# Routed experts with a softplus-gated FFN: VectorE splits, expert 7's block order and the queue of raw weight loads

## The chip, the cores and the metric

One Trainium2 chip; the kernel runs on one of its cores. The metric is device time in microseconds (us). Engines are named as in the profile: PE (TensorE), PEld (its weight loads), DVE (VectorE), ACT (ScalarE), POOL (GpSimd), SP (SyncE).

## The reference

Three steps, the middle and the last of which matter here:

```
x = attn(r, k, v, w, a, b)                    # a recurrence over 768 steps, 32 heads of 40
x: 3072 tokens x 320
logits = x @ w_gate + log1p(exp(x @ w_noise)) * noise          # 8 experts
top2   = the two largest of each row; weights = softmax over them
out[t] = sum over its two experts e of  weight * (relu(x[t] @ w1[e]) @ w2[e])    # 320 -> 1024 -> 320
h = out @ w_in                                # 320 -> 2048, w_in and w_out are given as float64
y = (h * tanh(softplus(h))) @ w_out           # 2048 -> 320
```

## The kernel before, in words

The program has three stages: the recurrence (`Rec`, to about 535 us), the experts (`Experts`, to about 983 us) and the final FFN (`Ffn`). Nearly all matmuls are of two operands that are each split into a high and a low part: `split` (L1084) makes the high part by a rounding copy on ACT and the low part by a subtraction, on DVE or, with `pool=True`, on POOL. A product is then three matmuls, high by high, high by low and low by high.

**Blocks.** Each expert has three blocks (`NS`) of its token list: 256 rows, 256 rows and, for the third, 256 or 384 rows, chosen at run time with `tc.If(n > BIG)` on the count of the expert (L1364 to L1371, `L1364` reads the count on every engine and `L1367` branches). Block j belongs to expert j // 3. `BLOCKS` (L754) is the order: 0, 1, 3, 4, 5, ..., 22, 23 and last 2, the third block of expert 0, for which expert 0's weights are loaded and split once more as unit 8. `p` counts places in this order.

**A block** (`block`, L1213). First layer: eight times eight matmuls (L1234) into `ph` (four buffers, each for two of the eight), then hh and hl out of it by `split` with relu (L1086 on ACT, L1088 on DVE). Second layer: for each 128 rows 24 matmuls (L1253), then the copy of y (L1259 on ACT) and at the end one store of y (L1267, SP). Between these instructions the block steps through generators, whose instructions are so woven into every engine's queue: `w2` splits the second weights of this expert in the first layer of its first block; `nxt` splits the first weights of the next expert during the second layers of the first and second block; `xt` transposes and splits the x of the next block; `more` is other work, `when` says how many steps of it are taken. `more` is the route's end (`late`, `table`) for the first experts and `Decode` for the third block of experts 1 and 2 and all blocks from expert 3 on.

**x of a block.** `ahead(p)` (L1297) issues the index load for place p + 3 (SP) and the gathers for place p + 2 (POOL, L1168), into one of three buffers, `xb[j % 3]`. Third blocks and block 2 share `xb[2]`. Block 2 stands right behind block 23 in the order, so its gathers are issued at the start of block 23 (`p + 1`), and its copy `twice` (L1201, DVE) is put behind the last hl of block 23 (`fresh=False`); otherwise the copy stands behind the first hl.

**The start** (`start`, L1279). `twice(0)`, three steps of the split of expert 0's w1 (L1179 on ACT, then L1181 and L1090), then the transposes and splits of block 0's x, a step of the route's end, and the other three steps of w1. `OPT['p1']` puts the first three w1 subtractions of expert 0 on DVE and the other three on POOL; its four w2 subtractions are on POOL (`OPT.get('pw', 1)`). For experts 1 to 7 and unit 8 the subtraction of the last 64 rows of w1 (L1181, two per expert) is on POOL, the rest on DVE. The route's end (`late`, `route`) is a chain of small DVE instructions (L857 to L975) with matmuls (L966, L967) in PE's order behind the third step of block 0's second layer.

**Zero stores.** `clear` (L1157) stores zeros over the rows of `yb` of each expert's possible third group of 128 and of the overflow blocks, by SP (L1160), three or four DMAs per expert, after its second block.

**Decode** (L1400). The float64 words of w_in and w_out come as pairs of int32. 44 items of 128x256 words, four steps each: step 0 issues the load of the next item's words (L1434, SP; 52 DMAs in all, as some items have two) and three DVE instructions (L1454 to L1456), steps 1 and 2 two more each (L1458, L1459; L1461, L1462), step 3 one on DVE (L1465), the cast on ACT (L1470) and two on POOL (L1471, L1472), and for w_out two stores (L1474, L1475, SP). There are two buffers of raw words.

Of the kernel before, what the change touches and what calls it, by code (L numbers as in the profile page):

```python
# [734 lines left out]
N, DM, NE, F = 3072, 320, 8, 1024  # L735
NT = N // 128
BT = 256
NS = 3
NBS = NE * NS
BIG = NS * BT  # L740
CAP = BIG + 128
# [9 lines left out]
LW = (2, 2, 2), (2, 2, 2)  # L751
EARLY = 2 * BT

BLOCKS = [0, 1, *range(NS, NBS), 2]  # L754
AT = {j: p for p, j in enumerate(BLOCKS)}
SHUT = 2
DFF = 2048
# [335 lines left out]
class Experts:  # L1093
# [78 lines left out]
    def split_w1(self, u, to=None):  # L1172
        nc = self.nc
        a = self.ld[u][0]
        h1, l1 = self.ws[u] = to or (self.w1h(), self.w1l())
        pool = iter(OPT['p1'] if u == 0 else (u <= NE, 0, 0) * 2)
        for c in range(0, F, 512):
            f = slice(c, c + 512)
            nc.scalar.copy(out=h1[0:64, 2, f], in_=a[0:64, 2, f])  # L1179

            (nc.gpsimd if next(pool) else nc.vector).tensor_tensor(out=h1[64:128, 2, f], in0=a[0:64, 2, f], in1=h1[0:64, 2, f].bitcast(F32), op=ALU.subtract)  # L1181
            yield
            for k in range(2):
                split(nc, a[:, k, f], h1[:, k, f], l1[:, k, f], pool=next(pool))
                yield
        if u + 1 <= NE:
            self.load_w1(u + 1)

    def split_w2(self, u):

        b = self.ld.pop(u)[1]
        for m in range(0, FC, 2):
            split(self.nc, b[:, m:m + 2], self.w2h[:, m:m + 2], self.w2l[:, m:m + 2], pool=u == 0 and OPT.get('pw', 1))
            yield
        if u + 1 <= NE:
            self.load_w2(u + 1)
# [13 lines left out]
            split(nc, pt, to[0][:, k, 0:128 * g], to[1][:, k, 0:128 * g])  # L1210
            yield

    def block(self, j, g, x, xt, nxt, more, when=(1, 1, 1), then=None, fresh=True):  # L1213


        nc = self.nc
        u = self.unit(j)
        h1, l1 = self.ws[u]
        h2, l2 = self.w2h, self.w2l
        w2 = self.split_w2(u) if u in self.ld else iter(())  # L1220
        n = 128 * g
        xh, xl = (t[:, :, 0:n] for t in x)
        hh, hl = (t[:, 0:FC * n].rearrange("p (m t) -> p m t", t=n) for t in (self.hh(), self.hl()))
        step = lambda it: next(it, None)
        for m in range(FC):
            c = 512 // n
            if m % c == 0:
                ph = self.ph()[:, 0:c * n].rearrange("p (c t) -> p c t", t=n)
            fs = slice(m * 128, m * 128 + 128)
            ops = [(h1[:, 2, fs], xh[:, 2]), (h1[:, 2, fs], xl[:, 2])]  # L1230
            for k in range(2):
                ops += [(h1[:, k, fs], xh[:, k]), (h1[:, k, fs], xl[:, k]), (l1[:, k, fs], xh[:, k])]
            for q, (a, b) in enumerate(ops):
                nc.tensor.matmul(ph[:, m % c], lhsT=a, rhs=b, start=(q == 0), stop=(q == len(ops) - 1))  # L1234
            if m % c == c - 1:
                split(nc, ph, hh[:, m + 1 - c:m + 1], hl[:, m + 1 - c:m + 1], relu=True)
            if m % 2:
                step(w2)
                if m == (1 if fresh else FC - 1) and then is not None:
                    self.twice(then)  # L1240
                for _ in range(when[0]):
                    step(more)
        for _ in w2:
            pass
        step(xt)
        step(xt)
        y = self.yt()
        for s in range(g):
            py = self.py()[:, 0:DM]
            ts = slice(s * 128, s * 128 + 128)  # L1250
            for m in range(FC):
                for q, (a, b) in enumerate(((hh, h2), (hh, l2), (hl, h2))):
                    nc.tensor.matmul(py, lhsT=a[:, m, ts], rhs=b[:, m], start=(m == 0 and q == 0), stop=(m == FC - 1 and q == 2))  # L1253
                if m % 3 == 2 and s < 2:
                    step(nxt)
                    for _ in range(when[1]):
                        step(more)
            step(xt)
            nc.scalar.copy(out=y[:, s], in_=py)  # L1259
            if s < 2:  # L1260
                step(nxt)
                for _ in range(when[2]):
                    step(more)
        for _ in xt:
            pass
        r = self.row(j)
        nc.sync.dma_start(out=self.yb[r:r + n, :].rearrange("(s p) d -> p s d", p=128), in_=y[:, 0:g])  # L1267
# [11 lines left out]
    def start(self, j, x, w, late=iter(())):  # L1279

        self.twice(j)
        for _ in range(3):
            next(w)
        for _ in self.xt(j, x):
            pass
        a, b = OPT.get('st', (1, 0))
        for _ in range(a):
            next(late, None)
        for _ in w:
            pass  # L1290
        for _ in range(b):
            next(late, None)
# [4 lines left out]
    def ahead(self, p):  # L1297

        if 1 < p < NBS - 3:
            self.load_ix(BLOCKS[p + 3])  # L1300
        for q in (p + 2,) * (p < NBS - 3) + (p + 1,) * (p == NBS - 2):
            if p != 2:
                self.load_x(BLOCKS[q])
        self.xts.pop(BLOCKS[p])
        x, self.xq = self.xq, (self.xh(), self.xl())
        j = BLOCKS[p + 1] if p + 1 < NBS else None
        return x, lambda: iter(()) if j is None else self.xt(j, self.xq), j

    def run(self, more, yg):
        nc, tc, rt = self.nc, self.tc, self.rt  # L1310
        none = iter(())
        self.zero = self.sb.tile([128, 160], F32, name="zero")
        nc.gpsimd.memset(self.zero, 0.0)
        late, table = rt.late(self.xb[2]), rt.table()

        def listed():
            yield from late
            next(table)
            self.load_ix(BLOCKS[4])
            self.load_x(BLOCKS[4])  # L1320
            yield
            self.load_ix(BLOCKS[5])

        first = listed()
        self.load_w2(0)
        self.xq = self.xh(), self.xl()
        self.start(0, self.xq, self.split_w1(0), first)
        for p, j in enumerate(BLOCKS):
            e, q, u = j // NS, j % NS, self.unit(j)
            if q == 0:  # L1330
                w = self.split_w1(u + 1)
            if q < NS - 1:
                x, xt, then = self.ahead(p)
                fill = first if e == 0 else table if e == 2 else none if e == 1 else more()
                self.block(j, 2, x, xt(), w, fill, OPT['lw'][q] if e == 0 else (1, 1, 1) if q == 0 else (1, 0, 1), then)
                if e == 0 and q == 1:
                    for _ in first:
                        pass
            if q == 1:
                for _ in w:  # L1340
                    pass
                if e == 2:
                    for _ in table:
                        pass
                    self.yg = yg()
                for d in range(ND * e // NE, ND * (e + 1) // NE):
                    self.clear(NE * CAP + d * BT, BT)
                self.clear(e * CAP + BIG, CAP - BIG)
                if e == 0:
                    self.clear(BIG - BT, BT)  # L1350
            if q < NS - 1:
                continue
            x, xt, then = self.ahead(p)
            fresh = p != NBS - 2
            if then is not None and fresh:
                self.twice(then)
                then = None
            if p == NBS - 1:
                m = nc.values_load(rt.last[0:1, 0:1], min_val=0, max_val=NBS + ND)
                self.rest(NBS, m, self.xq, (self.w1h(), self.w1l()))  # L1360

                for b in range(2):
                    expert_rows(nc, rt, self.yb, self.yg[b], b)
            n = nc.values_load(rt.cnt[0:1, e:e + 1], min_val=0, max_val=N)  # L1364
            kept, ld = dict(self.xts), dict(self.ld)
            at = more.at
            with tc.If(n > BIG) as big:  # L1367
                self.block(j, 3, x, xt(), none, more(), (2, 1, 1), then, fresh)
            with big.Else():
                more.at, self.xts, self.ld = at, kept, ld  # L1370
                self.block(j, 2, x, xt(), none, more(), (2, 1, 1), then, fresh)  # L1371
        for _ in more():
            pass

# [25 lines left out]
class Decode:  # L1400
# [29 lines left out]
    def load(self, i):  # L1430
        raw, src = self.raw[i % 2], self.todo[i][0]
        n = 128 // len(src)
        for k, a in enumerate(src):
            self.nc.sync.dma_start(out=raw[k * n:k * n + n], in_=a.rearrange("p (x w) -> p x w", w=2))  # L1434

    def __call__(self):

# [272 lines left out]
```

## Time and profile before

| | us |
|---|---|
| median of 3 runs | 1359.65 |
| lowest, highest | 1354.35, 1362.82 |
| the profiled execution | 1357.03 |
| its span in the trace | 1355.2 |
| mean granted clock of TensorE | 0.929 |

The span is what the instruction rows of the trace cover; the execution's own time has some 1.8 us around it. Rows name an engine, a line of the kernel (`L1253`), the operation, and tiles as out<-in without buffer numbers. In the view of waits a row says who was idle until whom, the time in all, how often, and the longest. In a timeline the bracket is the idle time just before and what ended it; neighbours of one kind are merged, with their count. A granted clock of 1.00 is 2.4 GHz and 0.50 is 1.2 GHz.

### The profile page before, as it was taken

How to read it: one execution, taken by the hardware profiler on the slowest of the kernel's cores; microseconds unless marked ns; L12 is line 12 of the kernel's file. 1: busy time of each engine (PE TensorE's matmuls, PEld its weight loads, DVE VectorE, ACT ScalarE, POOL GpSimd, SP SyncE). 2: the span in 40 equal slices, each digit the busy share in tenths (PEclk: the TensorE clock that was granted, in tenths of full speed). 3: DMA queues.
4: the chain of work that ended last, by engine and by line, in shares of the span. 5: the costliest groups of instructions: out<-in, count | busy, mean ns of one | idle time of the engine just before them, and what ended most of it. 6: DMA issues, size and time to landing. Idle time of an engine off the chain costs nothing. (4 is left out here: it accounts for less than half of the span.)

```text
span 1355.2 us, 34130 instructions
## 1 busy us (share of the span) xinstructions
PE 1168.1 (86%) x13902; PEld 1117.3 (82%) x13902; DVE 866.2 (64%) x1570; ACT 703.0 (52%) x1477; POOL 660.1 (49%) x584
## 2 busy tenths in 40 slices
PE   3436888888788897799998999897989999999998
PEld 2325777777677886698998999897989999999998
DVE  8595839486695652744786886765457565566543
ACT  3423675656456565342442443442366677666664
POOL 4693856657473514742243453443356455454431
PEclk9658898989699898899999999989999999999999
DMA  5444564555436547363444545645281111110000
GB/s 147 147 127 112 156 164 131 161 144 158 137 93 127 95 96 129 106 184 120 131 141 145 182 135 175 195 124 181 68 229 30 30 31 46 33 30 13 18 11 21
DMA packets 140898, 152.48 MB, mean 113 GB/s; under 512 B 69646, under 2 KB 112654, under 8 KB 140718
## 3 DMA queue, kind: packets, MB, share of 16 engines
q1 hardware_dynamic: 129966, 127.70, 34.7%
q0 software_dynamic: 10752, 22.32, 6.2%
q8 instruction: 120, 1.97, 0.7%
q14 instruction: 60, 0.49, 0.1%
HBM read 106.85 MB, written 43.12 MB: 111 GB/s over the span
## 5 line engine op out<-in xcount | busy, mean ns | idle before, releaser
L1582 POOL TENSOR_TENSOR gl<-fh,gh 128x1024 fp32r<-128x1024 f32 x46 | 131.0, 2875 | 105.7 <-ACT gh L1598 102.3
L1234 PE MATMUL ph<-xh,w1h 128*128 128x256 f32 (+1 forms) x576 | 160.8, 292 | 8.3 <-issue 4.8
L1234 PE MATMUL ph<-xl,w1h 128*128 128x256 f32 (+1 forms) x576 | 160.4, 291 | 0.1
L1550 PE MATMUL fps<-fxh,ih 128*128 128x256 f32 x576 | 156.4, 286 | 2.0 <-DVE fh L1552 2.0
L1550 PE MATMUL fps<-fxl,ih 128*128 128x256 f32 x576 | 153.8, 281 | 0.5 <-DVE fxl L1090 0.3
L1581 DVE TENSOR_TENSOR fh<-fh,fp 128x1024 f32<-128x1024 f32 x48 | 95.0, 2013 | 60.8 <-ACT fp L1580 60.8
L1253 PE MATMUL py<-w2h,hh 128*128 128x320 f32 x400 | 130.7, 327 | 1.4 <-ACT y L1259 0.8
L1253 PE MATMUL py<-w2h,hl 128*128 128x320 f32 x400 | 127.0, 318 | 5.5 <-DVE hl L1088 5.5
L1253 PE MATMUL py<-w2l,hh 128*128 128x320 f32 x400 | 126.5, 316 | 2.0 <-DVE w2l L1090 1.9
L1088 DVE SCALAR_TENSOR_TENSOR hl<-ph,hh 128x512 fp32r<-128x512 f32 (+1 forms) x104 | 69.1, 665 | 86.3 <-ACT hh L1086 85.9
L1234 PEld LDWEIGHTS ph<-xh,w1h 128*128 128x128 f32 x576 | 112.4, 195 | 9.2 <-issue 9.2
L1552 DVE COPY fh<-fps 128x512 f32<-128x512 f32 x96 | 64.7, 689 | 79.4 <-ACT fp L1551 73.9
L1612 PE MATMUL fpy<-oh,gl 128*128 128x320 f32 x384 | 114.6, 310 | 0.0
L1612 PE MATMUL fpy<-oh,gh 128*128 128x320 f32 x384 | 114.3, 310 | 0.0
L1612 PE MATMUL fpy<-ol,gh 128*128 128x320 f32 x384 | 113.9, 308 | 0.0
L1234 PEld LDWEIGHTS ph<-xl,w1h 128*128 128x128 f32 x576 | 112.4, 195 | 0.4 <-DVE xl L1090 0.4
L1234 PE MATMUL ph<-xh,w1l 128*128 128x256 f32 (+1 forms) x384 | 111.6, 291 | 0.0
L1550 PEld LDWEIGHTS fps<-fxh,ih 128*128 128x128 f32 x576 | 109.0, 189 | 2.4 <-DVE fh L1552 2.3
L1550 PEld LDWEIGHTS fps<-fxl,ih 128*128 128x128 f32 x576 | 109.0, 189 | 1.1 <-DVE fxl L1090 1.1
L1550 PE MATMUL fps<-fxh,il 128*128 128x256 f32 x384 | 107.8, 281 | 0.0
L1086 ACT ACTIVATE hh<-ph 128x512 fp32r<-128x512 f32 (+1 forms) x104 | 59.7, 580 | 87.6 <-PE ph L1234 87.2
L1551 ACT ACTIVATE fp<-fps 128x512 f32<-128x512 f32 x96 | 55.9, 596 | 79.2 <-PE fps L1550 75.1
(275 smaller groups left out, 3362.8 us busy)
## 6 DMA issues: line engine op xcount, KB each, us to landing
share<-in_w_dram SPq DMA_DIRECT2D x9, 1280.0 KB
share<-in_w_dram SPq DMA_DIRECT2D x9, 1024.0 KB
knd<-kn SPq DMA_DIRECT2D x24, 320.0 KB
KB<-knd SPq DMA_DIRECT2D x24, 320.0 KB
yb<-y SPq DMA_DIRECT2D x22, 320.0 KB
wa<-in_wa_dram SPq DMA_DIRECT2D x40, 162.7 KB
kb<-in_kb_dram SPq DMA_DIRECT2D x40, 160.0 KB
ST<-in_vn_dram SPq DMA_DIRECT2D x48, 128.0 KB
```

Source lines behind the costliest of these rows:

```text
L1086: nc.scalar.activation(out=hi, in_=src, func=AF.Relu if relu else AF.Copy)
L1088: nc.vector.scalar_tensor_tensor(out=lo, in0=src, scalar=0.0, in1=hi.bitcast(F32), op0=ALU.max, op1=ALU.subtract)
L1234: nc.tensor.matmul(ph[:, m % c], lhsT=a, rhs=b, start=(q == 0), stop=(q == len(ops) - 1))
L1253: nc.tensor.matmul(py, lhsT=a[:, m, ts], rhs=b[:, m], start=(m == 0 and q == 0), stop=(m == FC - 1 and q == 2))
L1550: nc.tensor.matmul(ph[:, i], lhsT=a, rhs=b, start=(q == 0), stop=(q == len(ops) - 1))
L1551: nc.scalar.activation(out=p[:, 2 * m2:2 * m2 + 2], in_=ph, func=AF.Sigmoid, scale=-1.0)
L1552: nc.vector.tensor_copy(h[:, 2 * m2:2 * m2 + 2], ph)
L1581: mul = lambda s: nc.vector.tensor_tensor(out=h[:, s], in0=h[:, s], in1=p[:, s], op=ALU.mult)
L1582: low = lambda s: (nc.vector if last and s.start % 8 else nc.gpsimd).tensor_tensor(out=gl[:, s], in0=h[:, s], in1=gh[:, s].bitcast(F32), o ...
L1612: nc.tensor.matmul(py, lhsT=a[:, m, ts], rhs=w[:, m], start=(q == 0), stop=(q == len(ops) - 1))
```

## The change

It has five edits. Expert 0's low parts of w1 and w2 and expert 1's low parts of w1 are all computed on DVE. Expert 7's blocks go in the order 21, 23, 22, so that block 2 stands behind block 22; the special cases for block 2's gathers and copy (`p + 1`, `fresh`) go. The zero stores move from behind an expert's second block to behind its first. The raw words of the FFN weights are loaded by ACT's queue. In `start`, the steps of block 0's x and of w1 alternate, with x ahead.

```diff
-BLOCKS = [0, 1, *range(NS, NBS), 2]
+BLOCKS = [0, 1, *range(NS, NBS - 2), NBS - 1, NBS - 2, 2]
...
-        pool = iter(OPT['p1'] if u == 0 else (u <= NE, 0, 0) * 2)
+        pool = iter((1 < u <= NE, 0, 0) * 2)
...
-            split(self.nc, b[:, m:m + 2], self.w2h[:, m:m + 2], self.w2l[:, m:m + 2], pool=u == 0 and OPT.get('pw', 1))
+            split(self.nc, b[:, m:m + 2], self.w2h[:, m:m + 2], self.w2l[:, m:m + 2], pool=False)
...
-                if m == (1 if fresh else FC - 1) and then is not None:
+                if m == 1 and then is not None:
                     self.twice(then)
...
         self.twice(j)
-        for _ in range(3):
+        for _ in self.xt(j, x):
             next(w)
-        for _ in self.xt(j, x):
-            pass
...
-        for q in (p + 2,) * (p < NBS - 3) + (p + 1,) * (p == NBS - 2):
-            if p != 2:
-                self.load_x(BLOCKS[q])
+        if p != 2 and p < NBS - 2:
+            self.load_x(BLOCKS[p + 2])
...
+            if q == 0:
+                for d in range(ND * e // NE, ND * (e + 1) // NE):
+                    self.clear(NE * CAP + d * BT, BT)
+                self.clear(e * CAP + BIG, CAP - BIG)
+                if e == 0:
+                    self.clear(BIG - BT, BT)
             if q == 1:
...
-                for d in range(ND * e // NE, ND * (e + 1) // NE):
-                    self.clear(NE * CAP + d * BT, BT)
-                self.clear(e * CAP + BIG, CAP - BIG)
-                if e == 0:
-                    self.clear(BIG - BT, BT)
...
-            self.nc.sync.dma_start(out=raw[k * n:k * n + n], in_=a.rearrange("p (x w) -> p x w", w=2))
+            self.nc.scalar.dma_start(out=raw[k * n:k * n + n], in_=a.rearrange("p (x w) -> p x w", w=2))
```

## Rows read from the trace of the kernel before

**Rows 1.** Windows: length; busy PE, PEld, DVE, ACT, POOL; PEclk; DMA share; GB/s

```profile
535.00:580.00 45.00, 33.36 (x253) 32.02 (x250) 32.09 (x93) 17.36 (x41) 32.23 (x41) 0.89 0.35 93
580.00:985.00 405.00, 377.65 (x2727) 370.96 (x2724) 267.70 (x652) 155.76 (x335) 152.88 (x163) 0.97 0.50 149
```

**Rows 2.** Waits of PE, 535 to 985 us: us in total, times, longest

```profile
PE py L966 <- DVE req L951: 7.8, 2, 6.6
PE pt L1209 <- DVE xl L1090: 6.3, 9, 2.4
PE pt L1209 <- DVE xb L1201: 6.1, 2, 5.5
PE py L1253 <- DVE hl L1088: 5.5, 5, 2.8
PE ph L1234 <- issue: 4.8, 1, 4.8
PE ph L1234 <- DVEq L1378: 1.9, 1, 1.9
...
PE ph L1234 <- ACT dhi L1470: 1.6, 1, 1.6
```

**Rows 3.** Timeline of DVE in block 0: start us, us, instruction

```profile
544.15 0.69 DVE L1088 SCALAR_TENSOR_TENSOR hl<-ph,hh 128x512 fp32r<-128x512 f32 x1 [3.81 <-ACT hh L1086]
...
545.79 1.10 DVE L858 TENSOR_SCALAR rskip<-rskip 128x2 f32<-128x2 f32 x1
...
548.90 6.55 DVE L929 TENSOR_TENSOR req<-rnoise,rm 128x32 f32<-128x32 f32 x1
555.48 1.30 DVE L931 TENSOR_TENSOR req<-req,c 128x32 f32<-128x32 f32 x1
...
557.70 0.19 DVE L929 TENSOR_TENSOR req<-rnx,rm 128x32 f32<-128x32 f32 x1
...
560.56 0.17 DVE L955 COPY rcs<-rcs 128x32 f32<-128x32 f32 x1
```

**Rows 4.** Timeline of POOL in block 0

```profile
549.26 6.13 POOL L1090 TENSOR_TENSOR w2l<-share,w2h 128x640 fp32r<-128x640 f32 x4
```

**Rows 5.** Groups by line and form, whole span: busy us, mean ns | idle

```profile
L1090 DVE TENSOR_TENSOR w2l<-share,w2h 128x640 fp32r<-128x640 f32 x32 | 26.7, 834 | 0.3
...
L1090 DVE TENSOR_TENSOR w1l<-share,w1h 128x512 fp32r<-128x512 f32 x34 | 26.0, 766 | 7.2 <-ACT w1h L1086 7.1
```

**Rows 6.** Timeline of SP's queue around the start of block 11

```profile
723.02 3.63 SPq L1160 DMA_DIRECT2D yb<-zero  x4
...
729.62 11.83 SPq L1434 DMA_DIRECT2D draw<-in_wi_dram  x6
```

**Rows 7.** Timeline of DVE in blocks 5, 11 and 23

```profile
628.02 0.29 DVE L1454 TENSOR_SCALAR de<-draw 128x256 int32<-128x256 int32 x1 [6.07 <-DMA draw<-in_wi_dram]
...
734.23 0.29 DVE L1454 TENSOR_SCALAR de<-draw 128x256 int32<-128x256 int32 x1 [4.52 <-DMA draw<-in_wi_dram]
...
946.27 0.29 DVE L1454 TENSOR_SCALAR de<-draw 128x256 int32<-128x256 int32 x1 [3.46 <-DMA draw<-in_wo_dram]
...
948.02 0.28 DVE L1201 COPY xb<-xb 128x192 f32<-128x192 f32 x1
```

**Rows 8.** Windows with a granted clock of 0.50, columns as in rows 1

```profile
557.10:563.90 6.80, 3.74 (x14) 3.61 (x15) 6.01 (x32) 0.00 (x0) 1.28 (x2) 0.50 0.52 184
632.20:635.60 3.40, 3.21 (x10) 2.42 (x10) 3.07 (x10) 0.91 (x3) 0.59 (x2) 0.50 0.02 7
738.00:741.40 3.40, 3.40 (x15) 3.40 (x15) 3.37 (x12) 1.11 (x3) 0.86 (x2) 0.50 0.12 44
...
946.30:953.00 6.70, 4.64 (x19) 4.64 (x20) 5.12 (x17) 1.37 (x3) 1.46 (x2) 0.50 0.20 72
```

**Rows 9.** Instructions of line L1434: min/median/max ns of an issue

```profile
L1434 SPq DMA_DIRECT2D draw<-in_wi_dram x32: 334/474/1166, 624.3 to 793.0; - x32
L1434 SPq DMA_DIRECT2D draw<-in_wo_dram x20: 333/384/1865, 801.8 to 944.0; - x20
```

More of the change, by code (lines that the diff above doesn't have):

```diff
@@ L1211, in xt, with block @@
             yield
-    def block(self, j, g, x, xt, nxt, more, when=(1, 1, 1), then=None, fresh=True):
+    def block(self, j, g, x, xt, nxt, more, when=(1, 1, 1), then=None):
         nc = self.nc
@@ L1353, in run @@
             x, xt, then = self.ahead(p)
-            fresh = p != NBS - 2
-            if then is not None and fresh:
+            if then is not None:
                 self.twice(then)
@@ L1367, in run @@
             with tc.If(n > BIG) as big:
-                self.block(j, 3, x, xt(), none, more(), (2, 1, 1), then, fresh)
+                self.block(j, 3, x, xt(), none, more(), (2, 1, 1), then)
             with big.Else():
                 more.at, self.xts, self.ld = at, kept, ld
-                self.block(j, 2, x, xt(), none, more(), (2, 1, 1), then, fresh)
+                self.block(j, 2, x, xt(), none, more(), (2, 1, 1), then)
         for _ in more():
```

## The prediction

> **What bounds the kernel now.** I read the windows first [rows 1]. Between 535 and 580 us, the start of the experts, TensorE is busy 33.4 of 45 us with a granted clock of 0.89 of full speed; from 580 to 985 us it is busy 377.7 of 405 us at 0.97. No other engine comes near that in the long stretch (VectorE 267.7, ScalarE 155.8). So TensorE sets the end there, and its idle time and its slow-clock time are what a change can win. In the waits of TensorE [rows 2] the reader is to see who ends that idle time: the route's L951 (7.8 us in 2 waits), the x copy L1201 (6.1 in 2, one of 5.5), hl (5.5 in 5), xl (6.3 in 9), 4.8 us of "issue" before a first layer, 1.9 for the register loads of L1378. Nearly all are VectorE's. Then the timelines of VectorE, GpSimd and SP say why VectorE was late, and the windows with the clock [rows 8] what each idle stretch cost beyond itself.
>
> Why L951 was late [rows 3, 4]: L929, an operation on 128x32, took 6.55 us from 548.90, while GpSimd ran four w2l subtractions for 6.13 us from 549.26. The same line at 557.70 took 0.19. L931 took 1.30 and L858 1.10. VectorE was not busy with work, it was held while GpSimd worked.
>
> Why hl and L1201 were late [rows 6, 7]: VectorE's queue stood at L1454, the first operation on raw FFN words, until they landed: 6.07 us at 628, 4.52 at 734, 3.46 at 946. At 734 SP issued the load only at 729.62, behind four zero stores (3.63 us) and a register load. hl stood behind L1454, and in expert 7's third block so did the x copy of block 2, for which TensorE waited 5.5 us.
>
> **The change, part by part.**
>
> *Splits on VectorE alone.* GpSimd loses three w1 pieces and four w2 pieces of expert 0 and two 64-partition pieces of expert 1. VectorE gets them at 0.77 and 0.83 us each [rows 5]. The three w1 pieces (3 x 0.77 = 2.3) and the first w2 piece (0.83) come before or just behind the first hl, before which VectorE sat idle for 3.81 us [rows 3]: hidden. Three w2 pieces come into the route's chain: 3 x 0.83 = 2.5 us. What goes is the hold: 6.55 - 0.19 = 6.36 at L929, 1.30 - 0.19 = 1.1 at L931, some 0.9 at L858, together 8.4. The chain from L858 at 545.79 to the last L955 (560.56 + 0.17 = 560.73) took 14.9; it becomes 14.9 - 8.4 + 2.5 = 9.0 and ends at 554.8. TensorE's L967 hangs on it, so the second layer goes on 5.9 us earlier. I take 5.6, as an hl now has to wait for ScalarE's hh here and there. Bounds: 2 (most of what goes comes back as waits for hl or w2l) and 7.8 (all of the L951 wait, rows 2). The half-speed stretch from 557.1 to 563.9, behind that idle time, I leave as it is: some 3.5 us of idle time stay, with a slow stretch of their own. The two expert 1 pieces (0.77 each) replace GpSimd pieces that held VectorE too: nothing, +-1.
>
> Here a rule of the Trainium skill reads otherwise. SBUF — State Buffer, section Who interferes with whom, says that a VectorE instruction with two SBUF inputs and a GpSimd instruction that reads SBUF exclude each other, for one whole instruction of the one that came first. By that, L929 would have been let in after one GpSimd piece, and 1.5 us would be won at L929 in place of 6.36. The row shows it held through four pieces; the row decides.
>
> *x split first.* Three w1 pieces used to stand between VectorE and the first xl. The first matmul starts up to 3 x 0.77 = 2.3 us earlier, but the chain above starts with the copy of block 1's x, which waits for a gather that the change doesn't touch. I take 0; bounds 0 and 2.3.
>
> *Raw words by ScalarE's queue.* 52 loads leave SP. A load is issued at its place in ScalarE's order, behind no zero store, y store or register load. On ScalarE's queue they cost 32 x 0.474 + 20 x 0.384 = 22.9 us of issue [rows 9], in a stretch where ScalarE is busy 155.8 of 405 us [rows 1]; what hides it is that it mostly waits for TensorE, with four ph buffers behind it. If that cover were gone, half a microsecond in each of some 17 blocks with decoding, 8 us, would show. The load waits for its buffer, whose last reader is L1461 of the item before; ScalarE's own cast of that item has already waited for a later VectorE instruction, so I expect no new wait. Behind a late one would stand hh, xh and the y copy, and TensorE for those. What goes: the hl waits of TensorE are 5.5 in all, the longest 2.8 [rows 2]; 5.0 of them I put down to blocks 5 and 11, which have the two longest waits for raw words, and 1.4 more of the xl waits that follow on the same delay (an estimate: two of the nine, 6.3 / 9 each): 6.4. Behind these waits the clock was granted at 0.50 (1.2 of 2.4 GHz) from 632.2 to 635.6 and from 738.0 to 741.4, 3.4 us each [rows 8], half of it lost: 3.4. Sum 9.8; I take 9.0. Bounds: -8 (the issue cost shows and nothing is won) and 11.
>
> Against it stands DMA: Bandwidth & Descriptors, section Issuing engines are not separate DMA queues, of the Trainium skill: issuing from another engine saves only the sequencer's issue time, as all run on the same 16 engines. By that rule only the wait in SP's queue goes and the time from issue to landing stays; the rival below gives that a time.
>
> *Expert 7's order first, third, second.* Block 2's x uses the same buffer as block 23's and could be gathered only once that was transposed, during block 23 itself; its copy was put behind the last hl. Now a whole block lies between gather and use, and the copy stands behind the first hl. The 5.5 us wait goes, and with it the half-speed stretch 946.3 to 953.0 behind it: the copy ended at 948.3 [rows 7], so 4.7 us of work at half speed, 2.3 lost. Sum 7.8. Bounds 3 (the branch stall grows) and 8. The 1.6 (L1470) before that block and the 1.9 at L1378 [rows 2] stay, they belong to the branches. What is late next is TensorE itself.
>
> *Zero stores one block earlier.* Three or four of SP's DMAs (3.63 us, rows 6) now stand before the index load and x gather of the second block, whose results are used a block later: hidden, 0. In the third block they no longer delay anything. If that cover is gone, 4 us once. A y store of a third block that has three groups overwrites cleared rows and waits for a store a block old.
>
> **Sum.** 5.6 + 0 + 9.0 + 7.8 = 22.4, less 1.0 for ScalarE's issues here and there: 21.4. The profiled execution took 1357.03 us (span 1355.2); less 21.4 is 1335.6. It is 2.6 below the median of the runs, 1359.65; the forecast for the median is 1338.2, say 1338.
>
> **Rivals.**
> 1. *The loads gain half.* By the mechanism of the second rule: the load at 729.62 was there for L1454 at 734.23, some 4.6 us [rows 7]. Issued by ScalarE some 3 us earlier (an estimate: the zero stores alone took SP 3.63), it is there at 731.2; VectorE wants it at 734.23 - 4.52 = 729.7. Then 1.5 of each wait stays, with its slow stretch. Of 9.0 some 3 is left, 1344; with nothing left, 1347. For it: the 16 engines are shared. Against: zero stores no longer run just then. 0.15.
> 2. *ScalarE becomes the one in the way (slower).* SP's six loads at 729.62 took 11.83 us [rows 6] where the issue of six takes 2.8: it waited some 1.5 us on each for a buffer. If ScalarE waits like that on 52 loads, that is 78 us with every hh behind it. It decides from where ScalarE falls back by more than the four ph buffers; if half comes through, +39, so 1338 + 39 = 1377. Against: the order above, by which the buffer is free. 0.06.
> 3. *The gains are taken back.* The third block's branch now comes right behind expert 7's first block. A first layer behind a branch waited 4.8 us for "issue" at one place [rows 2]; with a slow stretch like that of 946 behind it that is some 7.2. Two more of these leave 21.4 - 14.4 = 7.0: about 1353. 0.09.
> 4. *More than forecast.* The slow stretch at the start goes too (1.3), the second layers keep no other delay: 1329. 0.10.
>
> **How the numbers follow.** Forecast (1332 to 1344) 0.60. A measurement tells about 1% here, 13.6 us: faster means under 1346.05, slower over 1373.25. Faster: 0.60 + 0.10 + half of rival 1, 0.08 = 0.78. Within 1%: 0.07 + 0.09 = 0.16. Slower 0.06. The range runs from 1328 (all upper bounds but the smallest) to 1350, which takes in rival 1 and leaves out rival 2 and most of rival 3.
>
> **What would show it.** Right: L929 at 0.2 us with no GpSimd subtraction beside it; TensorE's wait for L951 3 to 4 us; "PE <- DVE hl" under 1 us; L1454 waiting under 5 us in all instead of three long waits; L1201 gone from TensorE's waits; granted clock 1.0 at the second layers of blocks 5 and 11 and around expert 7's end. Wrong: ScalarE's waits at L1434, or TensorE waiting for hh over 3 us; long waits still at L1454; "issue" over 6 us; a w2l or w1l wait of the second layer in expert 0.

## The result and the profile after

The changed kernel took 1342.73 us (median of 4 runs, 1340.16 to 1349.19) beside 1358.14 (1354.35 to 1362.82) of the kernel before: ratio 0.989, 95% interval 0.9855 to 0.9924, so 14.9 us less. The forecast was 1338, from 1328 to 1350. The profiled execution took 1343.39 us, its span is 1341.6.

Windows of the changed kernel, columns as in [rows 1] (the FFN now begins near 969):

```profile
535.00:580.00 45.00, 39.15 (x271) 37.06 (x269) 29.68 (x106) 19.02 (x44) 23.55 (x34) 0.89 0.50 121
580.00:972.00 392.00, 368.98 (x2695) 363.15 (x2694) 270.50 (x650) 154.44 (x331) 151.18 (x160) 0.98 0.50 151
```

TensorE is busy 39.2 of the first 45 us, against 33.4 [rows 1], at the same mean clock. Its waits in the experts, as in [rows 2]:

```profile
PE ph L1234 <- issue: 10.5, 3, 5.2
PE pt L1209 <- DVE xl L1090: 6.0, 8, 1.1
PE py L966 <- DVE req L951: 2.3, 2, 1.7
PE py L1253 <- ACT hh L1086: 1.9, 2, 1.3
PE py L1253 <- DVE w2l L1090: 1.9, 1, 1.9
PE py L967 <- DVE rcs L955: 1.6, 1, 1.6
PE py L1253 <- DVE hl L1088: 1.3, 3, 0.9
PE ph L1234 <- ACT ih L1467: 1.2, 1, 1.2
```

The waits that the prediction wanted gone are gone or small: L951 7.8 to 2.3, L1201 off the list, hl 5.5 to 1.3. But "issue" rose from 4.8 in one wait to 10.5 in three, and hh stands there with 1.9. Much of that rise is a change of name: the other two waits, 2.8 and 2.5 us at the branches into blocks 23 and 2, stood before under L1470 (1.6) and L1378 (1.9) [rows 2]. At the three branches together TensorE waited 8.3 us before and 10.5 after. VectorE's waits for raw words fell from 20.3 us in six to one (three lines up, L1454 is now L1451):

```profile
DVE de L1451 <- DMA draw<-in_wi_dram: 3.8, 1, 3.8
```

VectorE in block 0, beside [rows 3]:

```profile
545.94 0.23 DVE L1201 COPY xb<-xb 128x128 f32<-128x128 f32 x1 [2.57 <-DMA xb<-xd,ix]
...
548.42 0.19 DVE L929 TENSOR_TENSOR req<-rnoise,rm 128x32 f32<-128x32 f32 x1
548.65 0.19 DVE L931 TENSOR_TENSOR req<-req,c 128x32 f32<-128x32 f32 x1
...
554.10 0.17 DVE L955 COPY rcs<-rcs 128x32 f32<-128x32 f32 x1
```

L929 took 0.19 us in place of 6.55, and the chain ended at 554.3; the prediction had 554.8. Its first link waited 2.57 us for a gather in this execution, so that x first did not start it earlier.

For the experiments one measure is used throughout: the time between the first matmuls of two stretches in TensorE's timeline, which leaves the recurrence out. "Block 0" is from its first matmul to block 1's, "to FFN" from block 21's to the FFN's first transpose, "all" from block 0's to that transpose.

| profiled execution of | block 0 | block 5 | 10 and 11 | 19 and 20 | 21 to FFN | all |
|---|---|---|---|---|---|---|
| kernel before | 29.7 | 21.3 | 37.3 | 38.6 | 82.0 | 442.5 |
| changed kernel | 27.7 | 19.1 | 34.1 | 39.0 | 78.9 | 431.1 |
| after_again (the changed kernel) | 24.0 | 20.4 | 33.1 | 38.5 | 81.3 | 427.5 |
| u_split | 29.6 | 19.8 | 33.5 | 38.5 | 79.3 | 433.6 |
| u_start | 23.9 | 19.0 | 34.2 | 38.3 | 80.5 | 434.7 |
| u_loads | 25.3 | 20.2 | 35.8 | 39.5 | 81.7 | 433.8 |
| u_clear | 26.3 | 19.9 | 35.1 | 38.3 | 81.8 | 432.8 |
| u_order | 26.6 | 19.2 | 34.7 | 38.8 | 75.7 | 427.0 |
| w2late | 27.2 | 19.4 | 34.0 | 38.1 | 87.0 | 437.1 |
| old_w1late | 30.0 | 23.0 | 34.1 | 35.5 | 77.2 | 432.8 |
| only_order | 28.4 | 21.5 | 38.0 | 37.5 | 80.2 | 438.9 |
| only_loads | 29.6 | 21.2 | 37.0 | 38.5 | 76.7 | 433.2 |
| only_clear | 29.0 | 18.3 | 36.1 | 36.6 | 76.4 | 429.7 |
| old_w1e6 | 24.2 | 20.6 | 33.3 | 35.1 | 77.8 | 421.3 |

From before to after, 11.4 us went in the experts: 2.0 in block 0, 2.2 in block 5, 3.2 in blocks 10 and 11, 3.1 behind block 21, 0.9 elsewhere. The first matmul of the experts itself came 2.0 us earlier.

### The profile page after: what moved, and what is told of

Same layout as the page of the kernel before. It is cut to its first block, busy times and chain, and to the rows that moved or that the text cites. A ratio compares the mean times of both kernels' runs of the same rounds, so it can differ in the third digit from the quotient of the medians.

```text
span 1341.6 us, 34128 instructions
## 1 busy us (share of the span) xinstructions
PE 1160.1 (86%) x13902; PEld 1111.0 (83%) x13902; DVE 870.0 (65%) x1579; ACT 704.2 (52%) x1477; POOL 647.1 (48%) x575
## 5 line engine op out<-in xcount | busy, mean ns | idle before, releaser
L1234 PE MATMUL ph<-xh,w1h 128*128 128x256 f32 (+1 forms) x576 | 160.9, 292 | 11.6 <-issue 10.5
```

## The experiments

The experiments came in three groups, each on a chip of its own beside the kernel before: 1371.43 us for the first group (whose recurrence was some 14 us longer), 1359.95 for the second, 1358.82 for the third. So times are compared by ratio, and stretches by the table. The changed kernel itself was not run in the first group (u_split, u_start, u_loads, u_order). All four ratios there lie above its 0.989 and 0.9904, that of u_order too, whose experts lasted 427.0 us, no longer than after_again's 427.5. So a total of that group does not price an edit; its rows and stretches are what counts. Where the expectations say "blocks 9 and 10" or "block 18", they count places in the order; these are blocks 10, 11 and 19.

**One edit undone in the changed kernel.**

*u_split*: GpSimd takes its pieces back.

```diff
-        pool = iter((1 < u <= NE, 0, 0) * 2)
+        pool = iter(OPT['p1'] if u == 0 else (u <= NE, 0, 0) * 2)
...
-            split(self.nc, b[:, m:m + 2], self.w2h[:, m:m + 2], self.w2l[:, m:m + 2], pool=False)
+            split(self.nc, b[:, m:m + 2], self.w2h[:, m:m + 2], self.w2l[:, m:m + 2], pool=u == 0 and OPT.get('pw', 1))
```

> The changed kernel with one edit undone: the low parts of expert 0 (three w1 pieces, four w2 pieces) and of expert 1 (two pieces) are on GpSimd again. Theory (VectorE is held while GpSimd subtracts): L929 takes 4 to 7 us again beside the w2l pieces, the route's chain ends some 5 us later, and the part from the experts' first matmul to block 0's last second-layer matmul is 2 to 3 us longer than the changed kernel's 28.1 us (a late chain costs less than its own 6 us, since a half-speed stretch then lies on idle time): about 1345.5 us. Rival (the hold came from something else, such as the gathers of x that GpSimd issues there): L929 stays at 0.2 us, 1342.7. Second rival (the pieces on GpSimd also free VectorE for the rest): faster than 1342.

Measured 1363.26 us, ratio 0.994 (0.9916 to 0.9964). VectorE and GpSimd in block 0, from the timelines of this run:

```profile
561.20 6.13 DVE L929 TENSOR_TENSOR req<-rnoise,rm 128x32 f32<-128x32 f32 x1
```

```profile
561.15 6.13 POOL L1090 TENSOR_TENSOR w2l<-share,w2h 128x640 fp32r<-128x640 f32 x4
```

The small operation began 0.05 us behind the four subtractions and lasted exactly as long as all four. That settles the hold: the pieces are the only thing that differs. Which instruction is caught varies. In only_loads, below, with the pieces on GpSimd too, L929 took 0.19 us and the third instruction behind it was held:

```profile
549.15 6.55 DVE L936 TENSOR_TENSOR roh<-rfi,c 128x32 f32<-128x32 f32 x1
```

Block 0 took 29.6 us, as before. But "all" hardly tells the edits apart, because block 0 with the new splits and the new start took anything from 24.0 to 30.0 us in eight profiles (mean 26.4; the four with the pieces on GpSimd, u_split's and those of the third group that leave the start as it was, 28.4 to 29.6). Two things in the traces go with that scatter: in four of the eight the chain waits 2.5 to 4.9 us for the gather and in the other four at most 0.14, and of the time from the chain's end to block 1 between 0 and 9.9 us is granted at half speed.

*u_start*: three steps of w1, then x.

```diff
-        for _ in self.xt(j, x):
-            next(w)
+        for _ in range(3):
+            next(w)
+        for _ in self.xt(j, x):
+            pass
```

> The changed kernel with the old start: three steps of w1, then x of block 0. Theory (x first took 1.65 us off the first wait, but the chain behind it waits for its gather): the first wait for xl is 2.3 us again instead of 0.7, the end of block 0 moves by 0 to 1 us: 1342.7 to 1343.7. Rival (all of it stays): 1344.3 or more, with block 0's end 1.6 us later.

Measured 1365.66, ratio 0.9958 (0.9933 to 0.9983). TensorE's first wait for xl was 2.4 us again, not 0.7. Block 0 itself took 23.9. Block 1 lost 7 us against the others: ScalarE stood still for 5.5 us before an hh there, and the trace names no engine as the releaser ("remote"). Whether the start's order brings that about wasn't tried, so this run gives the first wait and no total for the edit.

*u_loads*: raw words by SP again.

```diff
-            self.nc.scalar.dma_start(out=raw[k * n:k * n + n], in_=a.rearrange("p (x w) -> p x w", w=2))
+            self.nc.sync.dma_start(out=raw[k * n:k * n + n], in_=a.rearrange("p (x w) -> p x w", w=2))
```

> The changed kernel with one edit undone: the raw FFN words are loaded by SP's queue again, the zero stores stay behind the first block. Theory (the place in SP's queue made the words late): VectorE's waits for draw come back to 10 us or more in all (3.8 in the changed kernel, 20.3 before), blocks 5 and 11 have second layers of 12 us or more instead of 11.2 and 7.5, and the time is 1347 to 1350. Rival (the zero stores' move alone did it): block 11 stays near 7.5 us and the time within 1.5 us of 1342.7. Second rival (ScalarE's issues cost something): the time falls to 1339 to 1341.

Measured 1365.80, ratio 0.9951 (0.9927 to 0.9975). Neither theory as it stood: VectorE waited 6.6 us for raw words, not 10 or more, and block 11's second layer took 7.5 us as in the changed kernel, not 12. So with the zero stores moved the loads may be on SP again and block 11 stays cured. Blocks 10 and 11 and the stretch to the FFN were 1.7 and 2.8 longer than in the changed kernel's first profile, and 2.7 and 0.4 longer than in its second. Whether the loads' own queue still earns something beside the early zero stores, this run leaves open.

*u_order*: first, second, third again, with block 2's special cases; the zero stores stay early.

```diff
-BLOCKS = [0, 1, *range(NS, NBS - 2), NBS - 1, NBS - 2, 2]
+BLOCKS = [0, 1, *range(NS, NBS), 2]
...
```

> The changed kernel with expert 7's blocks in the order first, second, third again and block 2's gathers and copy with their special cases; zero stores stay behind the first block. Theory: TensorE waits 5 to 6 us for the x copy L1201 of block 2 again, with a half-speed stretch behind it; the 2.8 us issue wait at the branch into block 23 shrinks to under 1.5, since unit 8's second weights are then loaded a block earlier; from block 21's first matmul to the FFN's first transpose 83 to 84 us instead of 78.9: 1346 to 1348. Rival (the new branch stall and the late hh took the gain back whole): 1342 to 1344.

Measured 1360.70, ratio 0.9918 (0.9881 to 0.9956). The theory fell: the stretch to the FFN was 3.2 us shorter than in the changed kernel, not 5 longer. TensorE waited for L1201 only 2.5 us, without a half-speed stretch:

```profile
903.60:979.30 75.70, 69.84 (x498) 68.39 (x497) 47.93 (x110) 28.82 (x60) 30.76 (x32) 1.00 0.45 133
```

The same stretch in the changed kernel, 2.8 us of it TensorE's wait at the branch into block 23:

```profile
890.20:969.00 78.80, 71.04 (x498) 69.72 (x497) 48.53 (x110) 28.84 (x60) 30.45 (x31) 0.98 0.43 126
```

The profiled execution, 1353.72 us, is 7.0 under this run's median, so the 75.7 may be on the short side, and the total shows no gain from the old order.

This left a new question: what had taken the wait for block 2's x away, if not the order?

**The changed kernel beside other variants of it.**

*after_again*: the changed kernel, unedited.

> The changed kernel itself, as the measure for the kernels run beside it. Theory: ratio to the kernel before 0.989 again (0.985 to 0.993), and from the experts' first matmul to the first of the FFN 431 us, give or take 3, of which the start of the experts (to block 1's second layer) varies by 2 and the rest by 1.

Measured 1346.68, ratio 0.9904 (0.9872 to 0.9936): the same gain on another chip. Its "all" is 3.6 us shorter, nearly all of it in block 0.

*u_clear*: zero stores late for experts 0 to 6.

```diff
-            if q == 0:
+            if q == (e < NE - 1):
                 for d in range(ND * e // NE, ND * (e + 1) // NE):
```

> The changed kernel with the zero stores behind the second block again for experts 0 to 6 (for expert 7 they must stay, since its third block comes second); raw words still by ScalarE's queue. Theory 1 (the loads' own queue cured the late raw words, as the prediction had it): block 11's second layer stays at 7.5 us and the time within 1.5 us of the changed kernel's. Theory 2 (the zero stores' place did it, since with the loads back on SP and the stores early block 11 already took 7.5): VectorE or ScalarE waits for raw words again around block 11, its second layer takes 10 us or more, the experts last 3 to 6 us longer. Third: the stores late only make the branch into the third block dearer, by 1 to 3 us each at two or three places.

Measured 1346.05, ratio 0.9892 (0.9875 to 0.9908). Block 11's second layer stays at 7.5 us, as theory 1 said, and u_loads had said the same of the other edit. So each of the two cures block 11 alone. Blocks 10 and 11 are 1 to 2 us longer than in the changed kernel, as theory 3 said, and the total doesn't move.

*w2late*: unit 8's second weights behind the branch into block 23.

```diff
...
-        if u + 1 <= NE:
+        if u + 1 < NE:
             self.load_w2(u + 1)
...
+                if m == 1 and j == NBS - 1:
+                    self.load_w2(NE)
```

> The changed kernel with unit 8's second weights (1.3 MB) loaded in the first layer of block 23, behind its branch, instead of just ahead of it. Theory (PE's branch into block 23 took 4.98 us because its instruction fetch stood behind that load in the DMA engines): the branch takes under 1.5 us, the issue wait of 2.8 us at block 23 goes with the half-speed stretch behind it, 3 to 4 us less in the experts than the changed kernel. Rival (the branch is dear of itself, because the code of the arm must be fetched): the wait stays at 2 to 4 us. Second rival: ScalarE's wait for a woh store in that block moves to another place and takes back 2 us.

Measured 1347.74, ratio 0.9902 (0.9879 to 0.9925). TensorE's wait there fell from 2.8 and 3.0 in the changed kernel's two profiles to 1.5 us, its branch instruction from 4.98 and 5.24 to 3.70: half of the theory. The second rival then took back far more than 2. In the changed kernel ScalarE's cast L1467 had waited 4.67 us for a store of its output buffer:

```profile
921.58 0.41 ACT L1467 CAST dhi<-dq 128x256 fp32r<-128x256 f32 x1 [4.67 <-DMA woh<-dhi]
```

That store stood on SP behind the four zero stores and landed late:

```profile
911.85 3.57 SPq L1160 DMA_DIRECT2D yb<-zero  x4
916.98 0.33 SPq L1471 DMA_DIRECT2D woh<-dhi  x1
```

Here it stands behind the weight load too, and the same cast waits 10.07 us, with hh behind it; TensorE waited 7.6 us for hh:

```profile
923.99 0.40 ACT L1469 CAST dhi<-dq 128x256 fp32r<-128x256 f32 x1 [10.07 <-DMA woh<-dhi]
```

*old_w1late*: old order, and the first weights of experts 3 to 7 and unit 8 loaded behind the branch of a third block.

```diff
-BLOCKS = [0, 1, *range(NS, NBS - 2), NBS - 1, NBS - 2, 2]
+BLOCKS = [0, 1, *range(NS, NBS), 2]
...
-        if u + 1 <= NE:
+        if u == 0 or u == 1:
             self.load_w1(u + 1)
...
+            if m == 1 and j % NS == NS - 1 and NS < j < NBS - 1:
+                self.load_w1(j // NS + 2)
...
```

> The changed kernel with expert 7's old order (as in the run with the order undone, whose experts lasted 427.0 us against the changed kernel's 431.1), and with the next first weights (1.3 MB) of experts 1 to 6 loaded in the first layer of the third block, behind its branch, instead of ahead of it. Theory (the fetch stands behind the weight load): the issue wait at block 20, 5 us in every run so far with a half-speed stretch behind it, falls under 1.5, and the stalls of 1 to 2 us around block 11 shrink; 6 to 10 us off, experts 417 to 421 us. Rival (the stall is the fetch's own): block 20 still waits 4 to 5 us, experts 426 to 428. Second rival: the weights now come too late for the next expert's split; TensorE waits for w1l at the third or fourth place behind, slower by 2 us or more.

Measured 1348.24, ratio 0.9893 (0.9847 to 0.9938). The wait at block 20 fell to 1.7, as the theory said, and blocks 19 and 20 lost 3 us; the total did not follow. Block 0 took 30.0 us by its scatter (here 4.9 of it the wait for the gather), and block 5 23.0, with VectorE waiting for raw words 9.5 us in all (3.8 in the changed kernel), 7.7 of it there: the raw loads were issued at 621.83, a weight load at 622.72, and the words were there at 630.87.

**One edit alone in the kernel before, and a better version.**

*only_order*: new order; expert 7's zero stores have to go behind its first block.

```diff
-BLOCKS = [0, 1, *range(NS, NBS), 2]
+BLOCKS = [0, 1, *range(NS, NBS - 2), NBS - 1, NBS - 2, 2]
...
```

> The kernel before with one edit alone: expert 7's blocks first, third, second (its zero stores go behind its first block, as they must then; those of the other experts stay). Measure: the time from block 21's first matmul to the first of the FFN, 81.9 us before. Theory 1 (the prediction's: the order is worth 7.8 us by itself): 73 to 76 us, time ratio 0.994. Theory 2 (the order only trades the wait for block 2's x against dearer branches and a late hh behind the zero stores, as the run with the order undone hints, 75.7 there against 78.8 in the changed kernel): 79 to 85 us, time ratio 0.998 to 1.002. Blocks 9 and 10 together stay at 37 us under both.

Measured 1356.37, ratio 0.9989 (0.9964 to 1.0013). Theory 2. The stretch to the FFN in the kernel before and here, and TensorE's only wait of note here:

```profile
900.50:982.40 81.90, 71.91 (x497) 70.52 (x496) 45.84 (x110) 28.91 (x60) 32.46 (x32) 0.96 0.41 126
901.00:981.20 80.20, 73.11 (x498) 72.63 (x497) 47.57 (x111) 28.98 (x60) 28.68 (x31) 0.94 0.41 127
```

```profile
PE ph L1234 <- issue: 7.1, 2, 4.7
```

The 5.5 us of L1201 are gone; the two branches took 7.1 us where they had taken 3.5 (1.6 and 1.9 [rows 2]), at a mean clock of 0.94 (0.96 before).

In this run VectorE was let in before GpSimd was through. Its first held instruction ended 0.05 us behind the third of the four w2l pieces, and the next waited for the fourth:

```profile
551.13 3.73 DVE L929 TENSOR_TENSOR req<-rnoise,rm 128x32 f32<-128x32 f32 x1
554.90 1.54 DVE L931 TENSOR_TENSOR req<-req,c 128x32 f32<-128x32 f32 x1
```

```profile
550.15 6.24 POOL L1090 TENSOR_TENSOR w2l<-share,w2h 128x640 fp32r<-128x640 f32 x4
```

*only_loads*: raw words by ScalarE.

```diff
-            self.nc.sync.dma_start(out=raw[k * n:k * n + n], in_=a.rearrange("p (x w) -> p x w", w=2))
+            self.nc.scalar.dma_start(out=raw[k * n:k * n + n], in_=a.rearrange("p (x w) -> p x w", w=2))
```

> The kernel before with one edit alone: raw words loaded by ScalarE's queue. Theory 1 (the late raw words were what held the x copy of block 2 as well as hl): from block 21 to the FFN 75 to 78 us instead of 81.9, with TensorE's wait for L1201 at 3 us or less in the old order; blocks 9 and 10 together 35 instead of 37.3; VectorE's waits for draw under 6 us in all instead of 20.3; ratio 0.993 to 0.996. Theory 2 (the x copy of block 2 was late because of its gather, and only the order cures it): 80 to 82 us there, ratio 0.997 to 0.999.

Measured 1351.05, ratio 0.9949 (0.9927 to 0.997), which is 6.9 us. Theory 1 holds for the end: 76.7 us with the old order, the clock at 1.00, L1201 at 2.4:

```profile
896.60:973.30 76.70, 69.87 (x498) 68.41 (x498) 48.09 (x110) 28.71 (x60) 30.80 (x32) 1.00 0.44 132
```

```profile
PE pt L1209 <- DVE xb L1201: 2.4, 1, 2.4
```

The waits for raw words came to 6.3 us. Block 11's second layer fell from 13.2 to 8.5 us; block 5 did not move (21.2), and blocks 10 and 11 together lost 0.3, not 2.

*only_clear*: zero stores behind the first block.

```diff
+            if q == 0:
+                for d in range(ND * e // NE, ND * (e + 1) // NE):
+                    self.clear(NE * CAP + d * BT, BT)
...
             if q == 1:
...
-                for d in range(ND * e // NE, ND * (e + 1) // NE):
-                    self.clear(NE * CAP + d * BT, BT)
...
```

> The kernel before with one edit alone: zero stores behind the first block. Theory 1 (the zero stores in front of the raw loads on SP made the words late, so that moving either cures it): block 11's second layer 7.5 instead of 13.2 us, VectorE's waits for draw 10 us or less in all, from block 21 to the FFN 76 to 79 us, ratio 0.993 to 0.997. Theory 2 (the prediction's: nothing): ratio 0.999 to 1.001, block 11 at 13 us.

Measured 1349.23, ratio 0.9934 (0.9909 to 0.996), which is 9.0 us for the edit that was priced at nothing. SP's queue at block 11, beside [rows 6]:

```profile
722.83 0.37 SPq L1267 DMA_DIRECT2D yb<-y  x1
723.64 0.37 SPq L1154 DMA_DIRECT2D ix<-ids  x1
725.47 15.60 SPq L1435 DMA_DIRECT2D draw<-in_wi_dram  x6
```

Without the zero stores the first raw load is issued 2.6 us after the y store. Before it was 7.0 us (y store at 722.61, load at 729.62), with 3.63 us of zero stores in between. Block 11's second layer takes 7.5 us, block 5 18.3, and the stretch to the FFN 76.4 at a clock of 1.00:

```profile
896.30:972.70 76.40, 69.93 (x498) 68.42 (x497) 47.30 (x111) 28.83 (x60) 31.10 (x32) 1.00 0.45 135
```

*old_w1e6*: the changed kernel with the old order, and unit 8's first weights alone behind the branch into block 20.

```diff
-BLOCKS = [0, 1, *range(NS, NBS - 2), NBS - 1, NBS - 2, 2]
+BLOCKS = [0, 1, *range(NS, NBS), 2]
...
-        if u + 1 <= NE:
+        if u + 1 < NE:
             self.load_w1(u + 1)
...
+            if m == 1 and j == NBS - 4:
+                self.load_w1(NE)
...
```

> The changed kernel with expert 7's old order, and with unit 8's first weights (1.3 MB) loaded in the first layer of block 20, behind its branch, and no other weights moved. Theory (the order costs 3 us, and the branch into block 20 is dear because its fetch stands behind that load): the issue wait at block 20 is 1 to 2.5 us instead of 4.8 to 5.2, from block 18's first matmul to block 21's 36 us instead of 39, from there to the FFN 75 to 77: some 6 us less than the changed kernel, ratio to the kernel before 0.984 to 0.988. Rival (what is saved there comes back as late second layers of blocks 20 and 21, as with all weights moved): 38 to 39 and 77 to 79, ratio 0.988 to 0.991.

Measured 1336.83 (1335.27 to 1341.02), ratio 0.9839 (0.9809 to 0.9868): faster than the kernel before by 21.9 us, and by its ratio also faster than the changed kernel, whose two ratios are 0.989 and 0.9904 (its interval overlaps that of the first and not that of the second). TensorE's first matmul of block 20 and SP's queue there:

```profile
865.74 0.36 PE L1234 MATMUL ph<-xh,w1h 128*128 128x256 f32 x1 [1.92 <-issue]
```

```profile
864.31 0.37 SPq L1269 DMA_DIRECT2D yb<-y  x1
864.79 0.41 SPq L1154 DMA_DIRECT2D ix<-ids  x1
866.42 0.54 SPq L1129 DMA_DIRECT2D share<-in_w_dram  x1
867.05 1.29 SPq L1130 DMA_DIRECT2D share<-in_w_dram  x1
```

And in the changed kernel:

```profile
872.21 0.55 PE L1234 MATMUL ph<-xh,w1h 128*128 128x256 f32 x1 [5.17 <-issue]
```

```profile
862.90 0.54 SPq L1129 DMA_DIRECT2D share<-in_w_dram  x1
863.53 0.54 SPq L1130 DMA_DIRECT2D share<-in_w_dram  x1
```

With the load issued before the branch TensorE waits 5.2 us (5.0 in u_order, whose kernel differs from this one by the load's place alone), with the load behind it 1.9. Blocks 19 and 20 lose 3.4 us against after_again and nothing comes back in block 20.

## Why the prediction was right, and where it was wrong

The time lay in the range, 4.7 us above the forecast: 14.9 us came where 21.4 were forecast, off a kernel before that this time took 1358.14 and not 1359.65. The terms behind it were less good than the sum, and that it came so near is in part luck: the zero stores, taken at 0, earn 9.0 alone, and the order, taken at 7.8, earns 1.5. The range's lower end does not follow from the bounds either: 7.8 + 11 + 8 off 1359.65 is some 1333, not 1328; and of the 9 us behind rival 4's 1329 only 1.3 are worked out.

- **Splits on VectorE alone.** The mechanism was right, and u_split shows it: the hold lasted 6.13 us, as long as all four pieces. It did so in four of the five profiles with the pieces on GpSimd; in only_order VectorE had a turn behind the third. One piece alone took 1.5 to 1.6 us. The rule of the Trainium skill (SBUF — State Buffer, Who interferes with whom) that the lock is for one whole instruction doesn't tell the length of this wait. The chain came out as worked: its end at 554.3 for 554.8. What failed is "The half-speed stretch ... I leave as it is". From the chain's end to block 1's first matmul, before, after and in after_again:

```profile
560.73:569.53 8.80, 7.95 (x43) 7.71 (x44) 5.28 (x22) 2.26 (x5) 5.82 (x11) 0.82 0.01 2
554.27:565.59 11.32, 10.47 (x44) 10.03 (x45) 6.72 (x24) 2.26 (x5) 7.35 (x12) 0.57 0.37 117
558.31:565.69 7.38, 6.53 (x44) 6.29 (x44) 6.59 (x24) 2.26 (x5) 4.01 (x7) 1.00 0.58 179
```

  The chain ended 6.5 us earlier. 2.0 of it is the earlier start of the experts, and 2.5 are lost behind the chain, where the same work took 11.3 us for 8.8: the half-speed stretch now lies on that work (mean clock 0.57), while before it lay mostly on idle time, 3.74 us busy of 6.80 [rows 8]. So block 0 gained 2.0 where 5.6 were forecast. That is one execution. In after_again, the same kernel, no slow stretch lay there (clock 1.00), the work took 7.4 us, and block 0 was 5.7 us shorter than before. Over all the starts the gain is some 3 (block 0 takes 29.3 on the mean of the five profiles with pieces on GpSimd, 26.4 on that of the eight).
- **x split first.** Taken as 0, bounds 0 to 2.3. TensorE's first wait fell from 2.37 to 0.71, and came back in u_start. A gain in the total is not shown. The experts' first matmul came 2.0 us earlier, but it moves by more than that from run to run: 537.9 to 541.7 us in six profiles with x first, 539.9 to 543.0 in four without (the first group left out). And where the chain waits for the gather, as here for 2.57 us, what was won ahead of it is lost again, as argued.
- **Raw words by ScalarE's queue.** The mechanism was right: alone it took VectorE's waits for raw words from 20.3 to 6.3 us and the time down by 6.9 (forecast 9.0). The step that failed is where it would show: block 5, which the term counted on, did not move (21.3 and 21.2 us), and the largest part, 5.3 us, came in a place the term did not name, the x copy of block 2.
- **Zero stores one block earlier: "hidden, 0".** Wrong, and the largest miss: 9.0 us alone. The row that shows it had been read [rows 6]: the raw load stood on SP behind the zero stores. Its whole wait was booked under the loads' own queue. Either edit takes the load out from behind the stores, and so u_loads and u_clear both keep block 11 at 7.5 us.
- **Expert 7's order, 7.8 us.** Wrong: 1.5 alone, not told apart from nothing, and beside the other edits some 3 us dearer in its stretch, though no total shows that. [Rows 7] had already shown why: the copy of block 2's x stood behind L1454, which waited 3.46 us for raw words. Raw words in time cure it in the old order, 82.0 to 76.7 or 76.4 us. The seven profiles with the new order took 78.9 to 81.8 (w2late, with its own delay, aside), the five with the old order and an edit for the raw words 75.7 to 77.8. What the traces show there is in part rival 3: the second weights of unit 8 are now issued right ahead of a branch, whose wait is 2.8 us in the profile shown (1.6 before), and the zero stores ahead of a store that ScalarE waits for.
- **The rivals.** Rival 3 (gains taken back at the branches) came true in small part; it had 0.09. "Issue" grew by 5.7 us, but the three branches together by 2.2 (8.3 to 10.5). Rival 1's mechanism did not: the waits for raw words left are 3.8 us at one place. Rival 2 came true once and by another cause: ScalarE was in the way, but waiting for a store of its own output, not at the loads. Of the signs named, "issue over 6 us" said so at once.

The terms 9.0, 0 and 7.8 were added as if each had its own wait. The three edits act in the main on one, the late raw words: alone they measure 6.9, 9.0 and 1.5, and together, with the start's share, 14.9.

Of the wait at the branch into block 20 the runs show that the weight load's place alone moves it, 5.0 (u_order) to 1.9 us (old_w1e6). A load ahead of a branch does not always cost that: at block 20 it was issued 0.6 to 1.4 us ahead, while at blocks 5, 8, 14 and 17 one of the same size was issued 2.4 to 11.4 us ahead, and TensorE waited 0.1 us or less. Whether the longer lead or the branch itself makes that difference was not tried. The Trainium skill, Runtime: NRT & Kernel Launch, section Instruction fetch mechanics, says that a taken branch to instructions that are not at hand costs a fetch by DMA before the engine goes on. Both waits agree with it. That this fetch stands behind the weights in the DMA engines is the reading that fits both; no run measured the fetch by itself.

What stays open: the 5.5 us of ScalarE in u_start, the rest of the wait at a branch (1.9 us with no weight load ahead of it), what makes the gather and the half-speed stretch of block 0 differ between executions, and how much of the 6.9 and 9.0 us is the same time, as no run has those two edits alone together.

## What to carry to other kernels

Before terms are added, ask of each late instruction how many of the edits would cure it: edits that act on the same wait share its price, and an edit priced at nothing can be the one that earns it. A stall's end is worth its idle time only if a half-speed stretch behind it goes as well; one that stays moves from idle time onto work. Look at several executions first: the same kernel had that stretch in one profile and not in another. Here a large load issued about 1 us ahead of a run-time branch delayed the branch; issue it behind, and then look who else stands behind it in that queue.

## What the runs showed of the hardware that was not expected

- TensorE's "issue" wait at the branch into block 20 was 4.1 to 6.1 us in eleven profiles with a 1.3 MB weight load ahead of it, 3.1 in a twelfth (only_clear), and 1.7 and 1.9 in the two with the load behind it.
- A store of 128x256 words issued on SP at 916.98, behind four zero stores, released ScalarE only at 921.58, 4.6 us later.
- The same start of the experts took 24.0 to 30.0 us from its first matmul to block 1's in eight profiles.
- A VectorE instruction of 0.19 us was held for 6.03 to 6.55 us, through four GpSimd subtractions in a row, in four profiles; in a fifth it got in behind the third, after 3.73.
